# RetNet and feed-forward kernel: zero products on TensorE and moved decays at the start

## The chip, the cores and the metric

The kernel runs on one core of a Trainium2 chip. The metric is the device time of one execution in microseconds (us). The engines of a core work side by side, each through its own instructions in order: TensorE (PE in the profile; PEld is its loading of weights), VectorE (DVE), ScalarE (ACT), GpSimd (POOL) and SyncE (SP), which here issues the DMAs.

## The reference

Two blocks follow each other. The first is a recurrent retention layer, for 4 batches, 8 heads, 768 tokens, head dimension 64:

```
for t in range(S):
    state = gamma * state + k[t] (outer) v[t]
    y[t]  = scale * q[t] @ state
```

where `gamma` is one number per head. The second is a feed-forward layer on the 3072 x 512 result x, with a leaky ReLU between two products (512 x 2048, 2048 x 512):

```
h = x @ w_in
g = maximum(0.01 * h, h)
out = g @ w_out
```

The weights come in 64-bit floats, which the kernel turns into fp32 itself.

## The kernel before

The recurrence is done in 6 chunks c of 128 tokens, for each batch b of 4. For one (c, b):

- `decay_v` (L132) multiplies v by the decay of each token and head, `gk`, in place, on GpSimd: one 128x512 instruction (L134).
- `score` (L142) makes k times q on TensorE (tile `ap`, L148), `masked` (L151) multiplies it with a triangular mask on VectorE (tile `am`, L153).
- `reads` (L167) multiplies q with the carried state (chunks after the first), `values` (L174) multiplies `am` with the decayed v, both into tile `yp`; `state` (L186) sums k times decayed v into another part of `yp`. `products` does the three.
- `taken` (L190) scales the result into x (L195) and renews the state `st` (L199, L200), on VectorE.

The weights come in pieces of 128x512 64-bit words. `powers(n)` (ScalarE, L283 to L286) and `mantissas(n)` (VectorE, L295, L297, L299) turn piece n into fp32; `mantissas` then issues the load of a later piece. The feed-forward products are done per unit of weights and chunk in a seven-product scheme (`seven`, L347, with sums and differences by `plus`, `minus`, `add_sums`, `differences`, L303 and L306). For the first unit and the first two chunks the eight-product form `direct` (L357, L366) is used: it is a generator whose four steps can be started one by one between other work. Its step k needs weight piece k; its last step is followed by the activations of g on ScalarE (L371).

The order of instructions on each engine is the order in which the program is written out (`manual_schedule`). Loads of the first inputs are issued by SyncE ahead of everything (L507 to L517): q and k of a batch first, then k and v. PSUM has two buffers of two banks for `ap` and `yp` (tag `att`) and four banks (tag `ff`) for the feed-forward products. The change lies in the order written out for the first two chunks (L528 to L596), and in `decay_v`. `scored(c, b)` stands for `decay_v`, `score` and `masked` in this order.

## Time and profile before

| | |
|---|---|
| median of 8 runs | 676.57 us |
| lowest, highest | 675.03, 677.16 us |
| the profiled execution | 676.22 us |
| its span in the profile | 674.3 us |
| PE busy | 660.7 us (98%) |
| DVE, ACT, POOL busy | 370.3, 162.5, 28.9 us |
| DMA | 49.11 MB, 73 GB/s over the span |

Times in the profile are in us from the start of the span. The row "PEclk" gives the clock that TensorE was granted, in tenths of full speed, in 40 equal slices of the span; a window's clock is a share of 1. A product of fp32 operands leaves two records on PE. An arrow reads "written tile <- read tiles"; in a list of waits it reads "waiting <- waited for", followed by the total, the number of times and the longest.

### The profile page before, as it was taken

How to read it: one execution, taken by the hardware profiler on the slowest of the kernel's cores; microseconds unless marked ns; L12 is line 12 of the kernel's file. 1: busy time of each engine (PE TensorE's matmuls, PEld its weight loads, DVE VectorE, ACT ScalarE, POOL GpSimd, SP SyncE). 2: the span in 40 equal slices, each digit the busy share in tenths (PEclk: the TensorE clock that was granted, in tenths of full speed). 3: DMA queues.
4: the chain of work that ended last, by engine and by line, in shares of the span. 5: the costliest groups of instructions: out<-in, count | busy, mean ns of one | idle time of the engine just before them, and what ended most of it. 6: DMA issues, size and time to landing. Idle time of an engine off the chain costs nothing.

```text
span 674.3 us, 9567 instructions
## 1 busy us (share of the span) xinstructions
PE 660.7 (98%) x4112; PEld 578.9 (86%) x4112; DVE 370.3 (55%) x563; ACT 162.5 (24%) x271; POOL 28.9 (4%) x29
## 2 busy tenths in 40 slices
PE   5899999999999999999999999999999999999997
PEld 4788888888888888888888888888888888888886
DVE  2888668988889775513633623553541444341342
ACT  2342555436342002211301221210221120221210
POOL 2300000000000110000100100100100000000000
PEclk9899999999999999999999999999999999999999
DMA  9921231231411544002101300301300000000001
GB/s 328 401 68 64 63 125 63 77 112 62 157 62 64 189 157 156 1 0 69 58 17 63 110 1 0 126 0 63 125 1 0 1 1 26 37 1 0 1 1 62
DMA packets 15305, 49.11 MB, mean 73 GB/s; under 512 B 1824, under 2 KB 1824, under 8 KB 15264
## 3 DMA queue, kind: packets, MB, share of 16 engines
q1 hardware_dynamic: 15264, 48.51, 20.5%
q8 instruction: 32, 0.52, 0.3%
q14 instruction: 9, 0.07, 0.0%
HBM read 42.21 MB, written 6.29 MB: 72 GB/s over the span
## 4 chain that ended last, share of the span: by engine, by line
PE 98%; DMA 1%; DVE 0%; issue 0%; POOL 0%; SPq 0%; DVEq 0%; POOLq 0%
PE B_o L347 12%; PE A_o L347 12%; PE C_o L347 12%; PE B_h L347 11%; PE C_h L347 11%; PE A_h L347 11%; PE D_o L347 6%; PE D_h L347 6%; PE d L366 5%; PE yp L174 4%; PE ap L148 3%; PE yp L167 2%; PE yp L186 1%; DMA kv<-in_kv_dram 1%; POOL kv L134 0%
## 5 line engine op out<-in xcount | busy, mean ns | idle before, releaser
L347 PE MATMUL A_h<-x,w 128*128 128x256 f32 x352 | 83.2, 380 | 0.0
L347 PEld LDWEIGHTS A_h<-x,w 128*128 128x128 f32 x352 | 67.1, 190 | 8.9
L347 PE MATMUL A_o<-g,w 128*128 128x256 f32 x288 | 68.0, 380 | 0.0
L347 PEld LDWEIGHTS A_o<-g,w 128*128 128x128 f32 x288 | 54.9, 190 | 7.3
L379 ACT ACTIVATE g<-g 128x512 f32<-128x512 f32 x66 | 40.2, 630 | 85.8 <-DVE g L303 85.8
L303 DVE TENSOR_TENSOR m<-m,B_o 128x512 f32<-128x512 f32 x16 | 11.0, 685 | 66.0 <-PE B_o L347 66.0
L303 DVE TENSOR_TENSOR m<-m,B_h 128x512 f32<-128x512 f32 x22 | 15.1, 686 | 57.7 <-PE B_h L347 57.7
L384 ACT COPY m<-A_h 128x512 f32<-128x512 f32 x22 | 12.8, 582 | 140.2 <-PE A_h L347 100.5
L195 DVE TENSOR_TENSOR x<-yp,dec 128x512 f32<-128x512 f32 x24 | 16.5, 688 | 48.9 <-PE yp L186 36.6
L347 PE MATMUL C_h<-t,w 128*128 128x256 f32 x176 | 42.2, 383 | 0.0
L347 PE MATMUL B_h<-x,w 128*128 128x256 f32 x176 | 42.2, 383 | 0.0
L347 PE MATMUL B_h<-t,w 128*128 128x256 f32 x176 | 41.6, 380 | 0.0
L347 PE MATMUL D_h<-t,w 128*128 128x256 f32 x176 | 41.6, 380 | 0.0
L347 PE MATMUL C_h<-x,w 128*128 128x256 f32 x176 | 41.6, 380 | 0.0
L134 POOL TENSOR_TENSOR kv<-kv,dec 128x512 f32<-128x512 f32 x19 | 22.3, 1175 | 445.7 <-DMA kv<-in_kv_dram 395.6
L153 DVE TENSOR_TENSOR am<-ap,mask 128x1024 f32<-128x1024 f32 x24 | 28.6, 1220 | 17.1 <-PE ap L148 17.1
L347 PEld LDWEIGHTS D_h<-t,w 128*128 128x128 f32 x176 | 33.5, 191 | 4.5
L347 PEld LDWEIGHTS B_h<-t,w 128*128 128x128 f32 x176 | 33.5, 190 | 4.5
L347 PEld LDWEIGHTS C_h<-x,w 128*128 128x128 f32 x176 | 33.5, 190 | 4.5
L347 PEld LDWEIGHTS C_h<-t,w 128*128 128x128 f32 x176 | 33.0, 190 | 4.9
L347 PEld LDWEIGHTS B_h<-x,w 128*128 128x128 f32 x176 | 33.0, 190 | 4.8 <-issue 0.3
L306 DVE TENSOR_TENSOR gd<-g,gd 128x512 f32<-128x512 f32 x48 | 35.5, 739 | 1.8
(103 smaller groups left out, 1054.8 us busy)
## 6 DMA issues: line engine op xcount, KB each, us to landing
raw<-in_weights_dram SPq DMA_DIRECT2D x31, 512.0 KB, 4.2
qk<-in_qk_dram SPq DMA_DIRECT2D x19, 512.0 KB, 4.2
kv<-in_kv_dram SPq DMA_DIRECT2D x19, 512.0 KB, 5.5
out_dram<-o SPq DMA_DIRECT2D x24, 256.0 KB, 2.1
in<-in_qk_dram SPq DMA_DIRECT2D x3, 512.0 KB, 10.7
in<-in_kv_dram SPq DMA_DIRECT2D x3, 512.0 KB, 10.7
o_in<-in_qk_dram SPq DMA_DIRECT2D x2, 512.0 KB, 9.8
o_in<-in_kv_dram SPq DMA_DIRECT2D x2, 512.0 KB, 10.3
```

Source lines behind the costliest of these rows:

```text
L134: nc.gpsimd.tensor_tensor(out=v, in0=v, in1=gk.unsqueeze(2).to_broadcast([128, H, D]), op=ALU.mult)
L148: nc.tensor.matmul(ps[:, j, a, :], lhsT=x[ts(j, 64), 1, a, :], rhs=x[ts(j, 64), 0, a, :])
L153: nc.vector.tensor_tensor(out=am.rearrange("p j a t -> p (j a) t"), in0=scores[c, b].rearrange("p j a t -> p (j a) t"), in1=mask.unsqueeze ...
L167: nc.tensor.matmul(ps[ts(i, 64), j, m, :], lhsT=st[b][ts(j, 64), a, :], rhs=x[ts(j, 64), 0, a, :], start=(m == 0), stop=False, skip_group_ ...
L174: nc.tensor.matmul(ps[ts(i, 64), j, m, :], lhsT=y[:, 1, 2 * a + j, :], rhs=am[:, j, a, :], start=(c == 0 and m == 0), stop=True, skip_grou ...
L195: nc.vector.tensor_tensor(out=blocks, in0=ps[:, :, 0 : HP // 2, :], in1=gq, op=ALU.mult)
L303: nc.vector.tensor_tensor(out=out, in0=a, in1=b, op=ALU.add)
L306: nc.vector.tensor_tensor(out=out, in0=a, in1=b, op=ALU.subtract)
L347: nc.tensor.matmul(ps[:, i, :], lhsT=block(w, sa)[:, k, ts(i, 128)], rhs=rhs[:, k, :], start=(first and i == 0 and n == 0 and k == 0), sto ...
L366: nc.tensor.matmul(banks[r][:, i, :], lhsT=block(2 * u, r + 2 * kh)[:, k, ts(i, 128)], rhs=x[:, 2 * kh + th, k, :], start=(step == 0 and i ...
L379: nc.scalar.activation(g[:, i], g[:, i], AF.Prelu, alpha=0.01)
L384: nc.scalar.copy(out=got["m1"], in_=ps)
```

## The change

Four things. A `[128, 256]` part of the still unused tile `t` is set to zero, read as 512 bf16 columns, and multiplied with itself into an unused bank (`idle`) 8, 6, 2, 2 and 1 times at five places of the start; nothing reads the result. The decays of batches 0 and 1 of the first chunk are done by VectorE instead of GpSimd, with the same instruction; those of all four batches of the second chunk by ScalarE, with 8 activations of 128x64 (one per head) each. The scores of batch 1 now stand ahead of the state sums of batch 0 on TensorE. In batches 2 and 3 of the first chunk some steps change places: the state sums of batch 2 go ahead of `direct`'s second step and the scores of batch 3 behind it, and `taken` of batch 2 goes ahead of the third `mantissas`.

```
-    def decay_v(c, b):
+    def decay_v(c, b, engine=nc.gpsimd):
         v = heads[c, b][1][:, 1]
-        nc.gpsimd.tensor_tensor(out=v, in0=v, in1=gk.unsqueeze(2).to_broadcast([128, H, D]),
-                                op=ALU.mult)
+        if engine is not nc.scalar:
+            engine.tensor_tensor(out=v, in0=v, in1=gk.unsqueeze(2).to_broadcast([128, H, D]),
+                                 op=ALU.mult)
+        else:
+            for h in range(H):
+                engine.activation(v[:, h], v[:, h], AF.Identity, scale=gk[:, h : h + 1])
...
     x, t = xs[0]
-    scored(0, 0)()
-    products(0, [0])
-    scored(0, 1)()
-    next_powers()
+    nothing = t[:, 0, 0, :].bitcast(BF16)
+    nc.vector.memset(t[:, 0, 0, :], 0.0)
+    idle = psum.tile([128, 2, N], FP32, tag="ff", bufs=4, name="idle")
+
+    def keep_busy(n):
+        for _ in range(n):
+            nc.tensor.matmul(idle.rearrange("p i n -> p (i n)"), lhsT=nothing[:, 0:128],
+                             rhs=nothing, start=True, stop=True, skip_group_check=True)
+
+    keep_busy(8)
+    score(0, 0)
+    masked(0, 0)
+    decay_v(0, 0, nc.vector)
+    keep_busy(6)
+    reads(0, 0)
+    values(0, 0)
+    score(0, 1)
+    decay_v(0, 1, nc.vector)
+    masked(0, 1)
+    next_powers()
+    state(0, 0)
     taken(0, 0, x)
-    products(0, [1])
+    keep_busy(2)
+    reads(0, 1)
+    values(0, 1)
+    state(0, 1)
     taken(0, 1, x)
     next_powers()
     next_mantissas()
     next_powers()
     load(1, 3)
-    scored(0, 2)()
+    keep_busy(2)
+    decay_v(0, 2)
+    score(0, 2)
+    keep_busy(1)
+    masked(0, 2)
     steps = direct(0, 0, x, parts[0][1], 0)
     next(steps)
     reads(0, 2)
     values(0, 2)
+    state(0, 2)
     next_mantissas()
     decay_v(0, 3)
-    score(0, 3)
-    state(0, 2)
-    next(steps)
-    next_mantissas()
-    masked(0, 3)
-    next_powers()
+    next(steps)
     taken(0, 2, x)
     next_mantissas()
-    next(steps)
+    score(0, 3)
+    masked(0, 3)
+    next_powers()
+    next(steps)
+    next_mantissas()
     reads(0, 3)
     values(0, 3)
     state(0, 3)
+    decay_v(1, 0, nc.scalar)
     run(steps, {})
     taken(0, 3, x)
...
+    def scored_later(b):
+        score(1, b)
+        masked(1, b)
+
     steps = direct(0, 0, x, parts[0][1], 1)
     next(steps)
-    scored(1, 0)()
-    next(steps)
-    scored(1, 1)()
+    scored_later(0)
+    decay_v(1, 1, nc.scalar)
+    next(steps)
+    scored_later(1)
...
     run(steps, {})
+    decay_v(1, 2, nc.scalar)
     next_powers()
...
-    scored(1, 2)()
+    scored_later(2)
     steps = direct(1, 0, x1, parts[1][1], 0)
     next(steps)
-    scored(1, 3)()
+    scored_later(3)
+    decay_v(1, 3, nc.scalar)
     next(steps)
```

In the new file the lines lie 1 to 39 further down: `decay_v` is L135 (VectorE, GpSimd) and L139 (ScalarE), the zero products L541, scores L152, masks L157, `reads` L171, `values` L178, `state` L190, `taken` L199 to L204, `powers` L287 to L290, `mantissas` L299, L301 and L303, `direct` L370 and its activations L375.

## The prediction

> **What bounds the kernel now.** I read the page first, for which engine is full and where it is not.

> ```profile
> PE   5899999999999999999999999999999999999997
> PEclk9899999999999999999999999999999999999999
> DMA  9921231231411544002101300301300000000001
> PE 98%; DMA 1%; DVE 0%; issue 0%; POOL 0%; SPq 0%; DVEq 0%; POOLq 0%
> ```

> TensorE is full in all slices but the first two and the last, and its clock is below full only in the first two. A gain can only come from the first 34 us, and it reaches the end of the span if TensorE then stays full. The list of TensorE's waits over the whole span says where it was not:

> ```profile
> PE ap L148 <- DMA qk<-in_qk_dram: 4.2, 1, 4.2
> PE yp L174 <- POOL kv L134: 2.4, 1, 2.4
> PE d L366 <- DVE w L299: 1.9, 1, 1.9
> PE yp L174 <- issue: 1.4, 1, 1.4
> ```

> These are all of them. After 18.90 us TensorE waits for nothing, so the end is 18.90 us plus its work, at the clock it gets. The chain of waits gives the order of the first part:

> ```profile
> 7.55 1.05 POOL kv L134
> ...
> 8.64 1.98 PE yp L174 x16
> 10.62 0.85 PE yp L186 x16
> 11.47 1.52 PE ap L148 x16
> 13.00 1.38 issue
> 14.37 1.09 PE yp L174 x16
> ...
> 18.90 3.55 PE d L366 x8
> 22.46 1.10 PE yp L174 x16
> ...
> 25.26 3.65 PE d L366 x16
> ```

> Two readings matter. The same work costs two prices: 16 records of L174 took 1.98 us at 8.64 and 1.09 at 14.37; one step of L366 (8 records) took 3.55 at 18.90, while two steps took 3.65 at 25.26. So TensorE ran at half clock until about 12.4 us, although the clock column still says 1.00 there, and again at 18.90. Windows cut at the clock's changes show the second stretch:

> ```profile
> 12.35:15.76 3.41, 2.03 (x44) 1.87 (x40) 2.15 (x3) 3.28 (x6) 0.00 (x0) 1.00 1.03 413
> 15.76:19.17 3.41, 1.53 (x23) 1.27 (x19) 3.06 (x6) 2.10 (x5) 1.04 (x1) 1.00 1.03 408
> 19.17:22.58 3.41, 3.41 (x10) 2.25 (x11) 3.27 (x5) 1.74 (x3) 1.16 (x1) 0.50 1.02 407
> ```

> The columns are the window, its length, the busy time of PE, PEld, DVE, ACT and POOL, the clock, DMA. A stretch of 3.41 us with TensorE busy 2.03 (60%) was followed by full clock, one with 1.53 (45%) by half clock for exactly one such stretch.

> **The change, part by part.** Some prices in the new order, as spacing between starts in the trace: scores 1.09 us, values 1.09, state sums 0.6, a step of `direct` 1.83 (3.65/2), a mask 1.23, `taken` 0.94 (15.97 to 16.91), `mantissas` 1.94 (16.91 to 18.85).

> *The first decays on VectorE.* A 128x512 multiply there takes 0.69 (rows L303, L306 at 685 to 739 ns) against 1.04 on POOL. The one of batch 1 now stands in front of mask (0,1) on VectorE, so the mask, and behind it `taken` and `mantissas`, wait for that batch's v. It landed at 10.73 at the latest: there POOL's decay of it began, released by the DMA:

> ```profile
> 10.73 1.04 POOL L134 TENSOR_TENSOR kv<-kv,dec 128x512 f32<-128x512 f32 x1 [2.14 <-DMA kv<-in_kv_dram]
> ```

> So the new chain runs from that landing: decay to 11.4, mask to 12.65, values (0,1) to 13.8, state sums to 14.4, `taken` to 15.4, `mantissas` of piece 0 to 17.3, first `direct` step at 17.4 instead of 18.90: **1.5 us**. `taken(0,0)` (12.65 to 13.6) hides beside values and sums. The other inputs must be early enough: mask (0,0) needs its scores. With the zero products ending near 4.9, scores at half clock take 2.08 to 7.0, mask to 8.2, decay to 8.9, values (0,0) to 10.0 and, with the second scores now ahead of the state sums, scores (0,1) to 11.1: just before 11.4. Half clock for values and scores as in the trace (1.98 and 1.52) would end them at 12.4, a delay of 1.0.

> *The products of zeros.* None is in the trace. There are 8 ahead of the first scores, 6 ahead of values (0,0), 2, 2 and 1 later, one pass over 512 bf16 columns each. The nearest row, one record of 256 fp32 columns, is 0.23 at full and 0.44 at half clock; twice the columns would be 0.46 and 0.89, the same time per record 0.23 and 0.44. I take the lower pair, assuming that a record's time goes with its operand's bytes (512 bf16 columns have those of 256 fp32 ones); no row decides that. Then 8 at half clock last 3.5 us, from about 1.35 (behind the memset at 0.90 that takes 0.17, and a second of some 0.25) to 4.9, 0.7 after the first q and k landed (4.20), which the 1.5 us above allow for. The later ones fill waits (2.4 and 1.4 us in the list) and cost nothing while those last. What they bring is the clock: the last 1.25 us before the first `direct` step stay idle (scores (0,2) and one product end at 16.2), so any 3.41 us stretch is at least 63% busy, above the 60% that kept the clock. The first step then takes 1.9 instead of 3.55: **1.65 us**.

> [...] The trace has 0.50 behind a gap of 1.88 us, so I go by the trace.

> *What is late next.* With step 0 at 17.4, values (0,2) end at 20.3, state sums at 20.9, step 1 at 22.8, scores (0,3) at 23.9. Step 2 needs `mantissas` of piece 2. On VectorE: mask (0,2) to 18.5, piece 1 to 20.5, `taken(0,2)` 21.0 to 22.0, then L295 of piece 2. POOL still decays batch 3, released by its DMA at 21.42, and in the trace that L295 took 1.27 instead of 0.42, until POOL was done:

> ```profile
> 21.42 1.32 POOL L134 TENSOR_TENSOR o_in<-o_in,dec 128x512 f32<-128x512 f32 x1 [4.54 <-DMA o_in<-in_kv_dram]
> 21.76 1.27 DVE L295 TENSOR_SCALAR w<-raw 128x512 uint32<-128x512 uint32 x1
> ```

> So piece 2 ends at about 24.55, as it did before, and step 2 waits from 23.9: **0.65 us given back** (0 if that collision does not recur, 1.3 if `taken` collides too). It starts at 24.55; before, it started at 25.26 + 1.83 = 27.09. That is 2.5 us in all (1.5 + 1.65 - 0.65). Its own scores, moved behind step 1, are masked by 25.8, before values (0,3) at 26.4.

> *Decays of chunk 1 by ScalarE.* Four POOL decays go, and with them their collisions with VectorE (L295 1.10 at 26.77, L306 1.53 at 33.44); that is worth little at the end, because TensorE does not wait there. In come 4 times 8 activations of 128x64. No row is that small: between an eighth of the 128x512 row (0.08) and all of it (0.63), a decay costs 0.6 to 5.0 us. VectorE's 0.42 for 256 and 0.69 for 512 elements leave 0.15 fixed; by that shape I take 0.25, 2 us a decay. [...] What is queued behind them: at 24 us, nothing before the activations of g at 29; at 31, the powers of pieces 4 and 5; at 44, the powers of 6 and 7. Values (1,0) and (1,1) come at 38.5, 11 and more after the landings; values (1,3) at 53.0. The last decay ends at 45.85 plus two decays, so it is hidden up to 3.6 us a decay, 0.45 each.

> DMAs keep their order; they are issued behind a queue full until 33 us, and nothing of the new order needs one earlier than that (batch 3 at 21.42 for 26.4). After 34 us all shifts together: 43.53 has VectorE waiting for TensorE, not the reverse.

> **Sum.** The profiled execution took 676.22 us, its span 674.3; minus 2.5 is 673.7. The median of the runs is 0.35 above that execution, so 674.0.

> **Rivals.** *The clock drops once more before the first `direct` step.* For it: 1.25 us idle there and score products that fill 64 rows of 128. Against: 60% busy kept it. The step begins at 17.4 and takes 3.55; values (0,2) end at 22.1, step 1 at 24.5, scores at 25.6, step 2 at 25.6 instead of 27.09: 1.5 gained, 675.1.

> *Zeros do not raise the clock, and are hidden.* Then the change does not do what it says: scores to 7.0, six zeros to 9.7, values cold to 11.7, scores to 13.5, mask to 14.75, step 0 at 19.4, half clock there as before: 0.5 later than now, 677.1. For it: no trace shows zeros. Against: the clock before followed busy time.

> *Zeros are slow and stand ahead of the real work* (slower). TensorE works in order. At 0.6 each at half clock, without raising it, 8 end at 6.15, scores at 8.2, six more at 11.8, values at 13.8, scores at 15.4, mask at 16.6, and through the same chain step 0 at 21.2: 2.3 later, 678.9. It decides from about 0.5 each. For it: twice the columns of a record. Against: the same bytes.

> **How the numbers follow.** Forecast 0.76, clock drops again 0.12, zeros without effect 0.06, zeros slow 0.06. This kernel's measurement can tell about 0.2%, 1.35 us. The second case lies at that bound, so half of it is counted as faster, and a little of the forecast's tail as the same: faster 0.80, same 0.13, slower 0.07. The range: up to 675.8, past the second case and a decay price near its bound; down to 672.8, with no give-back (0.65) and 0.5 for a half-clock stretch that differs from one execution to the next.

> **What would show it.** Right: first `direct` step at 17.3 to 17.6, 8 records in 1.9 us, clock 1.00 from about 9 us on, a TensorE wait near 24 us for VectorE's L303 (L299 before), no other after it. Wrong: records of zeros at 0.5 us and more, 0.50 in the clock after 17 us, values of chunk 1 waiting for ScalarE, or activations over 0.45 us.

## The result, and the profile after

The changed kernel takes 673.6 us (median of 12 runs, 673.11 to 675.02); the kernel before, measured beside it, 676.45 us (35 runs). The ratio is 0.996, with a 95% interval from 0.9952 to 0.9968: 2.85 us less, where 2.5 were forecast and the forecast time was 674.0. The profiled execution took 673.71 us, its span 672.0. From the page, the rows shown of before:

```profile
PE   7999999999999999999999999999999999999997
PEclk9999999999999999999999999999999999999999
DMA  8922231221422553002102200301300000000001
PE 97%; DMA 1%; DVE 1%; SPq 0%; issue 0%; DVEq 0%
```

TensorE is now full, at full clock, from the second slice on. All its waits over the span:

```profile
PE d L370 <- DVE w L303: 2.0, 1, 2.0
PE idle L541 <- DVE t L536: 1.4, 1, 1.4
PE yp L178 <- DVE am L157: 0.7, 1, 0.7
PE yp L178 <- DVE kv L135: 0.6, 1, 0.6
PE idle L541 <- issue: 0.2, 1, 0.2
```

The wait for q and k (4.2) and the one for GpSimd are gone, but the first `direct` step still waits for `mantissas` (L303 now), for as long as before. The timeline of the start shows what the zero products do (start, duration, engine, line):

```profile
1.39 3.59 PE L541 MATMUL idle<-t 128*128 128x512 bf16 x8 [1.39 <-DVE t L536]
4.91 2.08 PE L152 MATMUL ap<-qk 64*128 64x128 f32 x16
6.92 1.48 PE L541 MATMUL idle<-t 128*128 128x512 bf16 x6
8.99 1.09 PE L178 MATMUL yp<-am,kv 128*64 128x128 f32 x16 [0.59 <-DVE kv L135]
```

Eight take 3.59 us, six 1.48: 0.45 each at half clock, 0.25 at full. The clock rose at about 6.9 us instead of 12.35, so values (0,0) take 1.09 instead of 1.98. Then the chain of waits:

```profile
13.03 1.09 PE yp L178 x16
...
16.82 1.36 DVE w L303
18.18 0.04 issue
18.22 2.00 PE d L370 x8
20.22 1.02 PE yp L178 x16
21.24 0.47 PE yp L190 x16
21.71 1.92 PE d L370 x8
23.63 1.09 PE ap L152 x16
24.72 1.96 PE d L370 x8
26.68 1.02 PE yp L178 x16
27.70 0.47 PE yp L190 x16
28.17 3.65 PE d L370 x16
```

The first step starts at 18.22 (before: 18.90) and takes 2.00 (3.55); the third starts at 24.72 (27.09), the fourth at 28.17 (30.40). The 2.2 us of the fourth step are the 2.3 by which the span is shorter: after it nothing changes.

### The profile page after: what moved, and what is told of

Same layout as the page of the kernel before. It is cut to its first block, busy times and chain, and to the rows that moved or that the text cites. A ratio compares the mean times of both kernels' runs of the same rounds, so it can differ in the third digit from the quotient of the medians.

```text
span 672.0 us, 9626 instructions
## 1 busy us (share of the span) xinstructions
PE 663.4 (99%) x4129; PEld 578.0 (86%) x4131; DVE 370.2 (55%) x566; ACT 170.2 (25%) x303; POOL 21.7 (3%) x23
## 3 DMA queue, kind: packets, MB, share of 16 engines
q1 hardware_dynamic: 15264, 48.51, 20.5%
## 4 chain that ended last, share of the span: by engine, by line
PE 97%; DMA 1%; DVE 1%; SPq 0%; issue 0%; DVEq 0%
PE A_o L351 12%; PE B_o L351 12%; PE C_o L351 12%; PE B_h L351 11%; PE C_h L351 11%; PE A_h L351 11%; PE D_o L351 6%; PE D_h L351 6%; PE d L370 4%; PE yp L178 3%; PE ap L152 3%; PE yp L171 2%; PE yp L190 1%; DMA kv<-in_kv_dram 1%; DVE w L303 0%
## 5 line engine op out<-in xcount | busy, mean ns | idle before, releaser
L199 DVE TENSOR_TENSOR x<-yp,dec 128x512 f32<-128x512 f32 x24 | 16.5, 689 | 49.3 <-PE yp L190 37.0
L157 DVE TENSOR_TENSOR am<-ap,mask 128x1024 f32<-128x1024 f32 x24 | 28.6, 1220 | 12.9 <-PE ap L152 12.8
L351 PE MATMUL B_o<-gd,w 128*128 128x256 f32 x144 | 34.0, 380 | 0.0
## 6 DMA issues: line engine op xcount, KB each, us to landing
in<-in_qk_dram SPq DMA_DIRECT2D x3, 512.0 KB, 10.2
in<-in_kv_dram SPq DMA_DIRECT2D x3, 512.0 KB, 10.2
```

The costliest lines, as they stand in the source:

```text
L157: nc.vector.tensor_tensor(out=am.rearrange("p j a t -> p (j a) t"), in0=scores[c, b].rearrange("p j a t -> p (j a) t"), in1=mask.unsqueeze ...
L199: nc.vector.tensor_tensor(out=blocks, in0=ps[:, :, 0 : HP // 2, :], in1=gq, op=ALU.mult)
L351: nc.tensor.matmul(ps[:, i, :], lhsT=block(w, sa)[:, k, ts(i, 128)], rhs=rhs[:, k, :], start=(first and i == 0 and n == 0 and k == 0), sto ...
```

## The experiments

All times are medians; ratios are to the kernel before, run on the same chip beside each. Where the clock is the question, the granted clock of every execution is counted: one stretch of half clock (3.41 us) lowers the mean of an execution to 0.997. The three series of the kernel before that ran beside the experiments show 0.997 in 49 of 62 executions (median 676.5) and 1.0 in 12 (median 675.0: eight at 674.1 to 675.2, four at 677.5 to 678.5, of which no trace is kept). A mean of 0.999 is counted as no such stretch: in the two profiles that have it (e4, e6) the first `direct` step took 1.99 us, the time of full clock. (Behind the last product, which ends at 670.51 us in the kernel before and at 668.21 in the changed one, their clock records have half clock once more, from 674.53 and 672.57.) The mean leaves out half clock at the start: the clock column reads 1.00 until the first change, also where zero products take 0.45 us (the changed kernel, up to 6.97).

**e1, no zero products.** What is multiplied and its memset stay in the program; nothing is issued.

```
-        for _ in range(n):
+        for _ in range(0):
```

> The changed kernel without its 19 zero products; all decays and the new order stay. Theory (the gain is mostly the clock, bought by the zero products): scores at half clock from 4.2 to 6.3, values (0,0) at half clock to about 10.2, scores (0,1) to about 12, mask to 13.4, so the first direct step starts at about 18.8 instead of 18.2 and runs at half clock (3.5 us instead of 2.0): 676 to 676.6, within 0.1% of the kernel before. Rival (the new order and the moved decays carry the gain): first direct step at 18.2 to 18.4 at full clock, 673.6 to 674.3.

674.49 us (0.9983, 0.9974 to 0.9991). Neither: 4 of 12 executions have 0.997 (675.5 to 675.9), the others lie at 674.0 to 675.0. The profiled one is of the second kind. The chain of waits:

```profile
8.30 1.97 PE yp L178 x16
10.27 2.03 PE ap L152 x16
...
18.68 1.99 PE d L370 x8
```

The start is cold, as expected (1.97, 2.03), and the first step starts at 18.68, as expected; but it ran at full clock here, although TensorE had idled 2.2 us ahead of it; in the kernel before, the step ran at half clock behind 1.9 us. So the length of a gap alone does not decide in these two. By the clock record in the trace, full clock began at 14.09 here (the values (0,1), from 13.61 on, took 1.31 us, between the 1.97 of half and the 1.09 of full clock). Counted on from there in steps of 3.41 us, the stretches share the gap: 14.09 to 17.50 is busy for 2.38 us (70%), 17.50 to 20.91 for 2.23 (65%).

**e2, zero products alone.** The kernel before, with 8, 6, 2, 2 and 1 zero products ahead of scores (0,0), `products` of batch 0, `products` of batch 1, and around `scored(0, 2)`.

```
+    keep_busy(8)
     scored(0, 0)()
+    keep_busy(6)
     products(0, [0])
...
+    keep_busy(2)
     products(0, [1])
...
+    keep_busy(2)
     scored(0, 2)()
+    keep_busy(1)
```

> The kernel before with the same zero products (8, 6, 2, 2, 1) at the same places, and nothing else changed: all decays stay on GpSimd, the old order stays. Theory (clock): values (0,0) at 8.7 at full clock, scores (0,1) done at about 11.4, mask at 12.7, first direct step at about 18.0, in 2.0 us: 673.9 to 674.6, nearly all of the gain. Rival (decays and order are needed for it): 675 or more, with the second values waiting for GpSimd or for scores behind the state sums.

673.95 us (0.997, 0.9959 to 0.9981), none of 8 executions at 0.997; one of them took 1550.79 us with full clock, which nothing here explains (the ratio leaves it out). The theory holds. The chain of waits:

```profile
8.54 1.09 PE yp L174 x16
...
17.74 1.99 PE d L366 x8
```

With all decays still on GpSimd and the old order, the first step starts at 17.74, earlier than in the changed kernel. That holds to the end in this profile: the fourth step starts at 27.61 (changed kernel: 28.17), and the span is 671.5 us (672.0). So what the new order and the moved decays add to the zero products can't be told from nothing: 0.997 and 0.996, with intervals that overlap.

**e9, the new order alone.** No zero products, all decays on GpSimd at the places that the new order gives them.

> The changed kernel without zero products and with all decays back on GpSimd: only the new order of scores, state sums, masks and mantissas is left. Theory (the order by itself saves little; the products of zeros and the decays off GpSimd bring the rest): executions without a drop of the clock at 674.6 to 675.2, those with one at 676 to 676.8, median 675 to 676.5. Rival (the order brings the 1.7 that were left without zero products): median 674.3 to 674.7.

677.02 us (1.0006, 0.9996 to 1.0016): no gain, on the theory's side and above its range; 10 of 12 executions at 0.997 or less (676.4 to 678.2), the other two at 675.7 and 675.9. Its profile shows the first step at 19.07 and a collision ahead of the fourth, which I come to with e4. So the new order by itself brings nothing; e1's gain over it is that of the decays off GpSimd, fewer drops of the clock among it (4 of 12). It is 1.6 us by the ratios; the medians differ by 2.5, but were taken on two chips.

**e3, the first decays back on GpSimd.**

```
-    decay_v(0, 0, nc.vector)
+    decay_v(0, 0)
...
-    decay_v(0, 1, nc.vector)
+    decay_v(0, 1)
```

> The changed kernel with the decays of batches 0 and 1 of the first chunk back on GpSimd. Theory as predicted (the faster multiply on VectorE shortens the chain): values (0,1) 0.3 later, 673.9. Rival (the decay on VectorE stands ahead of the second mask, which then starts 0.6 late, at 11.76 instead of about 11.15): values (0,1) start at 12.4 instead of 13.03 and the first direct step at about 17.6 instead of 18.22, 673.0 to 673.4.

673.42 us (0.9964, 0.9952 to 0.9975), executions from 673.28 to 673.76, within the spread of the changed kernel: VectorE's faster multiply is worth nothing here. The timeline shows why:

```profile
10.87 1.04 POOL L135 TENSOR_TENSOR kv<-kv,dec 128x512 f32<-128x512 f32 x1 [2.10 <-DMA kv<-in_kv_dram]
11.05 1.23 DVE L157 TENSOR_TENSOR am<-ap,mask 128x1024 f32<-128x1024 f32 x1 [2.95 <-PE ap L152]
```

On two engines the decay and the mask run side by side; values (0,1) start at 12.38 instead of 13.03 and the first step at 17.63, as the rival said. It did not say what came of that: the third step starts at 24.50 instead of 24.72, because `mantissas` of piece 2 are late (TensorE waits 0.4 for them).

**e4, the second chunk's decays back on GpSimd** (`nc.scalar` left out in all four calls).

> The changed kernel with the decays of the second chunk back on GpSimd, at the places in the order where ScalarE has them. Theory as predicted (collisions of GpSimd with VectorE that TensorE does not wait for): 673.6, the same. Rival (the collision with the mantissas of piece 3 at 26 us now lies on the path): the fourth direct step waits 0.3 to 0.7 us, 673.9 to 674.4.

674.28 us (0.9975, 0.9965 to 0.9986), executions from 673.97 to 674.39: 0.7 more than the changed kernel by the medians, 0.5 in the profiled spans (672.5 and 672.0). The rival holds. The timeline:

```profile
26.98 1.04 POOL L135 TENSOR_TENSOR in<-in,dec 128x512 f32<-128x512 f32 x1 [1.37 <-DMA in<-in_kv_dram]
27.00 1.56 DVE L303 SCALAR_TENSOR_TENSOR w<-w,z 128x512 f32<-128x512 f32 x1
28.62 2.64 PE L370 MATMUL d<-x,w 128*128 128x256 f32 x11 [0.38 <-DVE w L303]
```

GpSimd's decay makes the last operation of `mantissas` 1.56 us long instead of 0.69, and the fourth step waits for it. It ends 0.54 us behind the multiply (28.02 and 28.56), which is most of its own 0.69.

**e7, the last three zero products left out** (the 2 and 1 around the scores of batch 2).

> The changed kernel without the last 2 + 1 zero products (those around the scores of batch 2); the first 16 stay. Theory (the clock is gated by stretches of 3.41 us that run free of the kernel, and by how much of one TensorE idles): the idle time ahead of the first direct step grows from 1.75 to 2.4 us; the step's start stays at 18.2; the executions fall into two groups, one at 673.6 and one with a lower granted clock at 675.2, the second holding a third to two thirds of them. Rival (the early products alone keep the clock): all at 673.6 with clock 1.0.

674.82 us (0.9974, 0.9962 to 0.9986). 10 of 12 executions have a lower clock: 8 at 0.997 (674.6 to 675.2), 2 at 0.995 (676.1, 676.4); the two at 1.0 took 673.0 and 673.3. Two groups, as the theory said, and more in the second than it said. The profiled execution is one of the two at 0.995; windows cut where its clock changed (window, length, busy PE, PEld, DVE, ACT, POOL, clock, DMA):

```profile
13.55:16.96 3.41, 1.62 (x32) 1.32 (x28) 2.77 (x5) 2.10 (x4) 1.23 (x1) 1.00 1.02 405
16.96:20.38 3.42, 2.74 (x7) 2.20 (x8) 3.28 (x5) 3.26 (x6) 0.08 (x1) 0.50 1.03 410
20.38:23.79 3.41, 3.41 (x33) 2.76 (x33) 0.20 (x1) 0.50 (x1) 1.04 (x1) 0.50 1.03 410
```

A stretch busy for 1.62 of 3.41 us (48%) is followed by half clock. The next is busy 2.74 (80%), and half clock stays for another one; here it ends behind a full one.

**e8, the gap filled**: 7 zero products instead of 1 behind the scores of batch 2.

> The changed kernel with 7 zero products instead of 1 behind the scores of batch 2, about 1.5 us that fill the idle time ahead of the first direct step. Theory: no execution has a lower clock, all at 673.2 to 674.0, the median as for the changed kernel. Rival (products of zeros there cost time, since TensorE works in order): 0.2 to 1 us more than the changed kernel.

673.58 us (0.9958, 0.9943 to 0.9974), all six executions at clock 1.0. They end before `mantissas` do: TensorE waits 0.3 instead of 2.0 us for L303. The theory holds, though single executions spread wider than it said (672.67 to 674.32); with one drop in 13 executions of the changed kernel, six without one don't show that it is safer.

**e5, the decay of batch 2 on ScalarE.**

```
-    decay_v(0, 2)
+    decay_v(0, 2, nc.scalar)
```

> The changed kernel with the decay of batch 2 of the first chunk on ScalarE instead of GpSimd. Theory (the first direct step starts at 18.22 instead of 17.55 because the last operation of mantissas, L303, takes 1.34 instead of 0.69 while GpSimd decays batch 2 at 16.33): L303 back to 0.69, first direct step at about 17.5; then step 2 waits for the mantissas of piece 2, held by GpSimd's decay of batch 3 at 21.42, so only part is kept: 673.1 to 673.5. Rival (the first step's start does not matter, or ScalarE's powers are now late): 673.6 or more.

674.19 us (0.9973, 0.9961 to 0.9986). L303 is back to 0.69 and the first step at 16.81 (17.5 was expected; the v of batch 1 landed at 10.39 here, 0.76 earlier than in the changed kernel), and the gain is lost again, as the rival said: the list of TensorE's waits has a new one.

```profile
PE yp L178 <- ACT o_in L139: 2.0, 1, 2.0
```

ScalarE works in order, and ahead of this decay stand the powers of piece 2, which waited for that piece's landing until 18.47; the decay ran at 20.37. The profiled execution is one of the two of 12 with a drop of the clock (676.3 us; the other ten lie at 673.45 to 674.37), and piece 2 landed late in it (at 17.55 in the changed kernel). So the 2.0 need not be the wait of a usual execution; e6 shows 0.6.

**e6, no collisions.** The first two decays on GpSimd, those of batches 2 and 3 on ScalarE, the powers of piece 3 ahead of the decay of batch 3.

> The changed kernel with the decays of batches 0 and 1 of the first chunk back on GpSimd (no wait ahead of the second mask), those of batches 2 and 3 on ScalarE (no collision of GpSimd with the mantissas), and the powers of piece 3 ahead of the decay of batch 3 on ScalarE. Theory: first direct step at about 17.0 instead of 18.2, step 2 at 23.4 instead of 24.7, 1.3 less than the changed kernel: 672.0 to 672.6. Rival (the chain is then bound elsewhere, by ScalarE's queue or a landing): 673 or more, with TensorE waiting for ScalarE at values (0,2) or (0,3).

673.87 us (0.9966, 0.9953 to 0.9979): the rival. First step at 16.47, but the decay of batch 2 at 18.71, behind the powers of piece 2; TensorE waits 0.6 us for it, and the third step starts at 24.67, as in the changed kernel.

**e10, that decay ahead of those powers.** e6 with one line moved up:

```
     next_mantissas()
+    decay_v(0, 2, nc.scalar)
     next_powers()
     load(1, 3)
     keep_busy(2)
-    decay_v(0, 2, nc.scalar)
```

> The kernel of e6_no_collisions with the decay of batch 2 ahead of the powers of piece 2 on ScalarE, so that it does not queue behind the landing of that piece. Theory (ScalarE's order was what cost e6 its gain): decay of batch 2 at 16 to 18 us, values (0,2) at about 18.3, step 2 at about 23.0 instead of 24.7, the rest follows: 671.8 to 672.6. Rival (the next bound comes at once, by the mantissas of piece 3, the landing of batch 3 or VectorE's sums): 673 or more.

672.46 us (0.994, 0.9927 to 0.9954), executions from 671.79 to 672.87. The theory holds, and this version beats both kernels: 1.1 us less than the changed one by the medians, 1.4 in the profiled spans (670.6 and 672.0). Timeline, then chain of waits:

```profile
15.84 2.02 ACT L139 ACTIVATE o_in<-o_in,dec 128x64 f32<-128x64 f32 x8
16.06 0.69 DVE L303 SCALAR_TENSOR_TENSOR w<-w,z 128x512 f32<-128x512 f32 x1
```

```profile
16.81 1.99 PE d L370 x8
...
23.30 1.96 PE d L370 x8
...
26.75 3.65 PE d L370 x16
```

L303 keeps its 0.69 us, and the fourth step starts at 26.75 instead of 28.17.

## Why the prediction was right, point by point

*The clock, 1.65 us: right in size, and it is where the gain comes from.* The first step took 2.00 instead of 3.55, 1.55 less. e2 shows that the zero products alone bring 0.997 of the time before, and e9 that the new order alone brings nothing. The comparison over all executions splits the gain roughly: the 12 of before with a mean clock of 1.0 have a median of 675.0, so about 1.4 of the 2.85 us come without a drop ahead of the first step, and the rest from drops that no longer occur (49 of 62 before, 1 of the 13 whose clock is on record after). The 1.4 still hold a gain from the clock, that of its earlier rise, which the mean does not count.

*Why the clock holds: wrong.* I put the idle time ahead of the first step at 1.25 us, by which no stretch would be under 63% busy. The step came later than I said, and the gap is 1.95 us in the waits (1.7 without the one zero product whose record is missing). A stretch cut to its worst shows it:

```profile
14.80:18.20 3.40, 1.46 (x18) 1.10 (x17) 3.26 (x6) 2.08 (x4) 1.29 (x1) 1.00 1.03 407
```

That is 43% in the records (50% with the missing one), near the 45% and 48% that half clock followed in the kernel before and in e7. The place of that window is my choice. The clock's changes lie 6.83, 3.41 and 651.95 us apart in the kernel before, 2, 1 and 191 times 3.413, and 665.60 in the changed one, 195 times; so stretches are counted on from a change in steps of 3.413 us. Full clock began at 6.97 us here by the clock record in the trace. Counted on from there, stretches end at 13.80, 17.21 and 20.63, and the gap from 16.5 to 18.2 is shared between two. They are 72% and 70% busy:

```profile
13.80:17.21 3.41, 2.46 (x40) 1.86 (x37) 2.54 (x6) 2.43 (x4) 0.88 (x1) 1.00 1.03 410
17.21:20.63 3.42, 2.41 (x16) 1.93 (x18) 3.28 (x5) 2.98 (x5) 0.41 (x1) 1.00 1.02 405
```

So by these windows it was the place of the stretches that kept the clock in this execution, not the 63% that I had counted on; 43% to 50% at the worst place, beside 45% and 48%, leaves next to no margin. The place differs from one execution to the next: behind the same eight products the clock rose at 6.97 us in the changed kernel and at 4.08 in e5, and the scores that follow took 2.08 us in the changed kernel, 1.83 in e3 and 1.59 in e4, where they take 1.16 at full clock. e7's two groups, of one program (0.995 or 0.997 in ten executions, 1.0 in two), agree with that. One of 13 executions of the changed kernel did lose clock (0.997), and took 675.02: the first rival, priced at 675.1, is what happens then.

*The shorter chain, 1.5 us: 0.7, and not through the decays.* e2, with the old order and the old decays, brings the first step forward by 1.16 (18.90 to 17.74), and e9, with the new order and no zero products, by nothing (19.07): the chain is shorter because its first links run at full clock, on which the prediction had rested 1.0 of its 1.5. In the sum, two terms were off. The v of batch 1 landed at 11.15 and not at 10.73 (other profiles show 10.39 to 11.08; it differs between executions). And L303 took 1.34 us: GpSimd's decay of batch 2 ran beside it.

```profile
16.33 1.29 POOL L135 TENSOR_TENSOR o_in<-o_in,dec 128x512 f32<-128x512 f32 x1 [14.90 <-DMA o_in<-in_kv_dram]
16.82 1.34 DVE L303 SCALAR_TENSOR_TENSOR w<-w,z 128x512 f32<-128x512 f32 x1
```

L303 ended 0.54 us behind the multiply (17.62 and 18.16), as in e4. I had looked for that collision at the next decay only, at 21.42. In the kernel before, `mantissas` began at 16.91, as GpSimd finished; moving them forward moved them into it. e5, e6 and e10, without that decay on GpSimd, have L303 at 0.69.

*The 0.65 given back: not there.* With the first step 0.8 later than I said, `mantissas` of piece 2 began at 22.69, after GpSimd's decay of batch 3 (21.42 to 22.46), and TensorE did not wait. The third step started at 24.72, where I had 24.55: the two errors cancel, and the sum was right for a reason that was half wrong. e3 shows the give-back that I meant: there the first step is 0.6 earlier, and the third only 0.2.

*First decays on VectorE: wrong.* I named the wait they add (the mask behind them) and still counted a gain; e3 shows none.

*Decays of the second chunk: the price right, the worth wrong.* Eight activations take 2.02 us (2.0 forecast), each 0.33 and overlapping. They are hidden. But I called the collisions that they remove worth little at the end; e4 measures 0.5 to 0.7 us.

*Zero products: right.* 0.45 at half and 0.25 at full clock, where I took 0.44 and 0.23; the rival with slow ones falls with that, and the one with zeros that do not count falls with the rise of the clock at 6.9 us.

Open: how much of e1's distance to e9 is the decays and how much the clock's chance, since landings, too, differ from one execution to the next.

## What to carry to other kernels

Where one engine is full to the end, look at its clock as well as its waits, and price a gap by what share of a 3.4 us stretch it may empty, in the worst place (in these runs half clock followed stretches that were 39% to 48% busy); filling it with products that nobody reads is cheap (e2: 19 of them brought 0.997, the new order by itself 1.0006). When a step is moved forward, look up what runs on the neighbouring engine at its new time, not at its old one. When work is moved to an idle engine that works in order, its place matters more than its price: e6 and e10 differ in the place of one line and by 1.4 us.

## What the runs showed of the hardware

```profile
16.10:19.52 3.42, 1.70 (x8) 1.44 (x8) 3.28 (x5) 2.20 (x4) 1.12 (x1) 1.00 1.02 405
```

What ends half clock stays open: it stayed behind a stretch that was 80% busy (e7, 16.96 to 20.38 us, products of fp32), and ended behind one that was 79% busy (e5, 0.66 to 4.08 us, products of zeros) and behind full ones (before, up to 12.35 and 22.58; after, up to 6.97; e7, up to 23.79). The clock column reads 1.00 before the first change also where TensorE was slower: the 16 records of scores that took 2.08 us there (before, from 4.21) took 1.16 later (from 15.86).

A 128x512 multiply on GpSimd and L303 on VectorE took longer where they met. Where GpSimd had begun first, L303 ended 0.54 or 0.55 us behind it, with 0.79 to 1.02 us of the multiply still to go as L303 began (after, e4, e7, e8, e9); so L303 took 1.34 to 1.56 us there instead of 0.69. Where VectorE had begun first, GpSimd's multiply took longer: 1.42 instead of 1.04 us in e9 at 21.49, beside L303 with its 0.69. L295 took 1.27 instead of 0.42 us in before at 21.76, beside GpSimd's multiply (21.42 to 22.74). The mask kept its 1.23 us beside GpSimd's decay in e3 (11.05 and 10.87).
